# First loads on three queues, later mixing weights behind the token transposes, and engine orders from a priority table

## Chip, cores, metric

The kernel runs on one core of a Trainium2 chip. The metric is device time in microseconds (us) of one execution, as the median of several runs. A profiled execution gives, besides its own time, a span from its first to its last instruction and a record of every instruction.

## What is computed

A transformer block of two parts on 2048 tokens of width 512: linear attention with 32 heads of 16, then a gated MLP that mixes over tokens. Cut to what matters:

```python
phi = lambda t: jnp.where(t > 0, t + 1, jnp.exp(t)) + 1e-06
def _A_ref(x, wqkv, wo):
    q, k, v = ...                                  # x @ wqkv, split into heads
    pq, pk = (phi(q), phi(k))
    kv = jnp.einsum('bhsd,bhse->bhde', pk, v)
    z = jnp.einsum('bhsd->bhd', pk)
    num = jnp.einsum('bhqd,bhde->bhqe', pq, kv)
    den = jnp.einsum('bhqd,bhd->bhq', pq, z)[..., None] + 1e-06
    return (num / den) ... @ wo
def _B_ref(x, w_in, w_sp, b_sp, w_out):
    z = _gelu(jnp.einsum('bsd,df->bsf', x, w_in))
    z1 = z[..., :Fh]                               # Fh = 896
    z2 = _layernorm(z[..., Fh:], axis=-1)
    g = jnp.einsum('ts,bsf->btf', w_sp, z2) + b_sp[None, :, None]
    return jnp.einsum('bsf,fd->bsd', z1 * g, w_out)
h = x + _A_ref(_layernorm(x, axis=-1), A_wqkv, A_wo)
h2 = h + _B_ref(_layernorm(h, axis=-1), B_w_in, B_w_sp, B_b_sp, B_w_out)
```

All inputs and the output are bfloat16. The mixing weights `w_sp` are 2048 by 2048.

## The kernel before

Five engines run at once: TensorE (PE) for matmuls and transposes into PSUM, VectorE (DVE), ScalarE (ACT), GpSimd (POOL), and SyncE (SP), which here only issues transfers. Each engine takes its instructions strictly in order; an instruction whose input is not there holds up all behind it.

**Tiles and stages.** The 2048 tokens are 16 tiles of 128; two tiles are a pair, four a group. The stages are:

1. *First half.* x and the three weights wq, wk, wv (512 by 512 each) are loaded. Every tile gets its layer norm: statistics (L557) and an aggregate (L561) on DVE, Ln and Exp on ACT (L571, L573) for the inverse deviation, and the normalisation on DVE (L585) into one of four `xn` buffers. The normalised tile is transposed into `xT`: by PE, with a copy out of PSUM on ACT (L622, L627), or by a transposing transfer that SP issues (L611). `XDMA` says from which pair on it is SP. Then PE computes K and V of a pair (L654), eight matmuls of 512 columns each, and Q of a group, two feature blocks at a time (L680), eight matmuls. `phi` of K and Q is an Exp on ACT (L633) and two DVE operations (L634, L641); V is copied by ACT (L668).
2. *Sums over tokens.* 64 short matmuls (L703) give K times V and the sums of K; DVE masks and transposes them (L715 to L723), and four matmuls with wo give a combined matrix `mw` (L733).
3. *Denominators and out-projection.* The denominators of each group (L753) go through Ln and Exp on ACT, which is a reciprocal (L757, L760). They are spread over the features: by matmuls for the first group (L792), by matmuls and ACT copies into the store of the attention weights for the others (L770, L776). DVE multiplies (L796), PE multiplies with `mw` (L825), DVE adds to x (L830), which is then h.
4. *Second layer norm and z.* Statistics as above; the inverse deviation is a power on POOL (L578, L580). The first pair's tiles are transposed by PE, the other 14 by SP, into `hT`. PE computes the second half of z for each tile (L853: four matmuls of 512 and four of 384 columns), ACT applies Gelu (L862). The statistics of z are made on DVE (L877) for the tiles with `n % 4 < ZD`, and otherwise by ACT with a Square (L869) and small POOL operations. DVE normalises. The first half of z, `z1`, is computed transposed (L898), with a Gelu on ACT (L903).
5. *Mix and output.* For each of four groups of output tokens and seven feature blocks, 16 matmuls with the mixing weights (L926), then bias and gate on DVE (L932, L935); seven matmuls per tile for the output (L944), the sum with h (L950) and the store (L952).

The mixing weights come transposed from memory, by 16 transposing transfers on SP for each group (`wsp0` to `wsp3`, L504). `wsp3` uses the store of the attention weights, so it can be loaded only late. A transfer that SP issues for a token tile stands in the same queue.

**What sets the order.** Nothing is ordered by hand. Each operation is recorded with an engine, an estimated cost and a priority. `schedule` then goes through the work like a list scheduler: for each engine it computes when each ready operation could start and takes the one with the best priority among those that start at once. The order, the PSUM banks and the buffers of the pools come out of that, and waits are made for what the order needs. A constant of 0.1 us says how much later a better operation may start; every transfer is costed on its issuing engine's own queue. The scheduler's times are estimates made while building; on the chip only the order is left of them.

The loads stand in SP's queue in this order: x0, x1, wk, the pair x2 and x3, wv, and six more pairs of x; then transposes of `wsp0`. POOL loads wq after its constants, then wo, win and wout, each after the one before has landed, since POOL's transfers are chained.

Of the kernel before, what the change touches and what calls it, by code (L numbers as in the profile page):

```python
# [10 lines left out]
P = 128  # L11
# [98 lines left out]
class Program:  # L110
# [3 lines left out]
    ENGINES = ("pe", "act", "dve", "pool", "sp")  # L114

    def __init__(self, nc):
        self.nc = nc
        self.ops, self.writer, self.readers = [], {}, {}
        self.pools = {}
        self.groups = {}  # L120

    def op(self, eng, cost, fn, r=(), w=(), prio=None, after=(), dma=None, nbytes=0, lag=0.0):
# [32 lines left out]
        return o  # L155


    def _slot(self, tile):
# [14 lines left out]

    def schedule(self):
        for o in self.ops:
# [15 lines left out]
        while left:  # L191
            pick = None
            for e in self.ENGINES:
                best = None
                for o in cand[e]:
                    t = free[e]
                    for p in o.deps:
                        same = p.eng == e and p.grp is None
                        t = max(t, p.end + (0.0 if same and (e == "pe" or p not in o.raw) else 0.08))
                    self.now = t  # L200
                    ok = True
                    for tl in o.tiles:
                        if tl.slot is None:
                            s = self._slot(tl)
                            if s is None:
                                ok = False
                                break
                            t = max(t, s[2] + 0.08)
                    if not ok:
                        continue  # L210
                    key = (t if t > free[e] + 0.1 else free[e], o.prio, o.seq)
                    if best is None or key < best[0]:
                        best = (key, o, t)
                if best is not None and (pick is None or best[2] < pick[2]):
                    pick = best
# [17 lines left out]
            if o.grp is not None:  # L233
                dma_free[o.eng] = max(dma_free.get(o.eng, 0.0), t + 0.3) + o.bytes / 300e3
                o.end = max(dma_free[o.eng] + 1.2, t + 2.0)
            for tl in o.tiles:
# [119 lines left out]


def bass_sequential_preLN__linear_attn_block__mixer_gmlp__prompt_kernel(
    nc: bass.Bass,
# [19 lines left out]
    assert D == 512 and KD == 4 and NG == 4 and FH == KF * P and 512 < FH <= 1024  # L379
    WARM, XDMA, HDMA, LNACT = 10, 5, 1, 2  # L380
    DB, DC, SPP, PK, ZD = 6, 7, 14, 0.3, 1
    ONES, SCP, Q3P, NQ1 = 1, 7, 8, 4
# [104 lines left out]
    def load(eng, name, dst, src, nbytes, prio=None, whole=False, after=()):  # L487
        return op(eng, max(0.5, nbytes / 300e3) if eng == 'sp' else 0.8, lambda e: e.dma_start(dst.ap(), src), w=[dst], dma=(name, whole), nbytes=nbytes,
                  prio=prio, after=after)

    w3 = A_wqkv.rearrange("(c p) f -> p c f", p=P)
    load("sp", "x0", x[0, :], x_dram[0:P, :], P * D * 2)
    load("sp", "x1", x[1, :], x_dram[P:2 * P, :], P * D * 2)
    load("sp", "wk", wk.all(), w3[:, :, D:2 * D], D * D * 2)
    for p in range(1, NP):
        load("sp", f"x{p + 1}", x[2 * p:2 * p + 2, :],
             x_dram[2 * p * P:(2 * p + 2) * P, :].rearrange("(n p) d -> p n d", p=P), 2 * P * D * 2)
        if p == 1:
            load("sp", "wv", wv.all(), w3[:, :, 2 * D:3 * D], D * D * 2)

    def load_wsp(tg):
        for st in range(NT):
            dst = wsp[tg][st, :]
            op("sp", 1.3, lambda e, dst=dst, st=st: e.dma_start_transpose(  # L504
                dst.ap(), B_w_sp[tg * GW:(tg + 1) * GW, st * P:(st + 1) * P]),
               w=[dst], dma=(f"wsp{tg}", True), nbytes=3 * P * GW * 2, prio=5000)

    for tg in range(3):
        load_wsp(tg)

# [19 lines left out]
       r=[bmask.all()], w=[bmask.all()])  # L530


    op("pool", 0.1, lambda e: e.memset(zc.all().ap(), 0.0), w=[zc.all()])
    op("pool", 0.5, lambda e: e.memset(sel.all().ap(), 0.0), w=[sel.all()])
# [58 lines left out]
    for grp in LN1:  # L593
# [6 lines left out]
        for i, n in enumerate(grp):  # L600
            t = xn_t[n] = Tile(XN)
            o = normalise(t(), x[n, :], Row(st_x, n), 6, rs[i:i + 1], 10 * (n // 2) - 18)
            if n == 5:
                load("pool", "wq", wq.all(), w3[:, :, 0:D], D * D * 2, after=[o])
                load("pool", "wo", wo.all(), A_wo.rearrange("(c p) f -> p c f", p=P), D * D * 2, after=[o])

    def transpose_pair(p, src, dstT, prio, by_dma, single=1):
        if by_dma:
            for n in (2 * p, 2 * p + 1):
                a, d = src[n], dstT[:, n * P:(n + 1) * P]  # L610
                op("sp", 1.3, lambda e, a=a, d=d: e.dma_start_transpose(d.ap(), a().ap()), r=[a()], w=[d],  # L611
                   dma=(f"t{dstT.store.name}{n}", False), nbytes=3 * P * D * 2, prio=prio)
            return
# [300 lines left out]
    load("sp", "bsp", bsp(), B_b_sp.partition_broadcast(P), P * S * 2)  # L914
    load_wsp(3)
    G0 = Z0 + 100
# [46 lines left out]

    g.schedule()

# [53 lines left out]
```

## Time and profile before

| what | us |
|---|---|
| three runs | 253.45, 254.6, 259.03 (median 254.6) |
| the profiled execution's own time | 256.33 |
| its span, first to last instruction | 254.6 |
| first K matmul (L654) | 6.77 |
| wq lands, first Q matmul (L680) | 16.84, 16.89 |
| 64 short matmuls (L703) | 54.53 to 58.32 |
| first denominator matmul (L753) | 58.60 |
| first z matmul (L853) | 68.33 |
| last wait of PE ends; 88 z1 matmuls follow | 111.63 |
| mix begins | 130.62 |
| last output projections (L944) | 239.40 to 251.65 |

PE's clock was granted in full (1.00) throughout. The page's costliest group is the mix; its rows look like this:

```profile
L926 PE MATMUL ps<-wsp,pk_v_z 128*128 128x512 bf16 x336 | 73.0, 379 | 0.0
L633 ACT ACTIVATE e<-ps 128x1024 bf16<-128x1024 f32 x16 | 16.3, 1020 | 7.7 <-PE ps L680 4.3
```

A row has the line, the engine and operation, output and input with their shapes, the count; then busy us and the mean ns of one; then the idle time ahead of these instructions and what ended most of it. A matmul's 379 ns is its time in the pipeline; 336 of them take 73.0 us, because they overlap. The chain of waits goes back from the last instruction to whatever released it, step by step; here it is read in order of time. In the windows, each row is a stretch of time with the busy time of PE, PE's weight loads, DVE, ACT and POOL, then PE's granted clock, the share of the transfer engines in use and GB/s.

### The profile page before, as it was taken

What the parts mean: (1) busy time and instruction counts of PE and PEld (TensorE: products, weight loads), DVE (VectorE), ACT (ScalarE), POOL (GpSimd) and SP (SyncE); (2) the same over time, 40 slices, a digit from 0 to 9 for tenths busy, and PEclk for the clock granted to TensorE, in tenths of its full rate; (3) what the DMA queues carried; (4) which work ended last, traced back from release to release, by engine and by line L of the source; (5) the groups of instructions that cost most, each with busy time, mean ns of one, the idle gap of its engine ahead of it and who ended that gap; (6) DMA issues with size and microseconds to landing.
All of it is one profiled execution on the core that took longest, in us unless ns stands there. A gap on an engine that the chain in (4) does not pass through costs nothing.

```text
span 254.6 us, 3142 instructions
## 1 busy us (share of the span) xinstructions
PE 243.0 (95%) x1222; PEld 111.6 (44%) x1222; DVE 133.1 (52%) x253; ACT 89.3 (35%) x129; POOL 28.2 (11%) x74
## 2 busy tenths in 40 slices
PE   7879899999889999999999999999999999999995
PEld 3334344464334444444444444444444444444442
DVE  3797894698999799232003332243333433223443
ACT  3648655646876668897540000000000000000000
POOL 7311000001024536322000000000000000000000
PEclk9999999999999999999999999999999999999999
DMA  6979973548944454444410000002000010000022
GB/s 188 334 173 174 304 149 88 83 101 198 207 105 97 96 89 101 104 101 92 104 37 3 0 0 0 0 3 82 0 0 3 23 59 0 3 0 0 0 82 82
DMA packets 52206, 20.78 MB, mean 82 GB/s; under 512 B 46208, under 2 KB 51328, under 8 KB 52192
## 3 DMA queue, kind: packets, MB, share of 16 engines
q1 hardware_dynamic: 51392, 16.79, 31.2%
q0 software_dynamic: 800, 3.80, 5.5%
q8 instruction: 9, 0.15, 0.3%
q14 instruction: 5, 0.04, 0.1%
HBM read 7.47 MB, written 2.10 MB: 38 GB/s over the span
## 4 chain that ended last, share of the span: by engine, by line
PE 75%; DVE 11%; DMA 6%; ACT 4%; POOL 2%; issue 2%; POOLq 0%; ACTq 0%
PE ps L926 38%; PE ps L944 10%; PE ps L898 8%; PE ps L654 7%; PE ps L680 5%; PE ps L853 5%; DMA wqkv_wsp<-in_A_wqkv_dram 4%; DVE xh L830 3%; DVE small L557 3%; DMA hT<-xn 2%; DVE xT_pq_z L796 1%; ACT e L633 1%; ACT wqkv_wsp L776 1%; PE ps L622 1%; PE ps L825 1%
## 5 line engine op out<-in xcount | busy, mean ns | idle before, releaser
L926 PE MATMUL ps<-wsp,pk_v_z 128*128 128x512 bf16 x336 | 73.0, 379 | 0.0
L932 DVE TENSOR_TENSOR r<-ps,e 128x512 bf16<-128x512 f32 x28 | 19.4, 691 | 78.8 <-PE ps L926 78.8
L926 PEld LDWEIGHTS ps<-wsp,pk_v_z 128*128 128x128 bf16 x336 | 32.9, 98 | 39.6
L654 PE MATMUL ps<-wqkv_wsp,xT_pq_z 128*128 128x512 bf16 x128 | 29.2, 379 | 2.1 <-ACT xT_pq_z L627 1.0
L853 PE MATMUL ps<-win,hT 128*128 128x512 bf16 (+1 forms) x128 | 25.9, 352 | 1.5 <-DMA hT<-xn 1.1
L898 PE MATMUL ps<-hT,win 128*128 128x512 bf16 x112 | 25.0, 379 | 0.0
L944 PE MATMUL ps<-wout,xT_pq_z 128*128 128x512 bf16 x112 | 24.7, 379 | 0.0
L926 PE MATMUL ps<-wqkv_wsp,pk_v_z 128*128 128x512 bf16 x112 | 24.3, 379 | 0.0
L557 DVE BATCH_NORM_STATS2 small<-xh 128x6 f32<-128x512 bf16 x32 | 21.4, 678 | 4.7 <-DMA xh<-in_A_x_dram 4.5
L654 PEld LDWEIGHTS ps<-wqkv_wsp,xT_pq_z 128*128 128x128 bf16 x128 | 11.9, 98 | 17.7 <-ACT xT_pq_z L627 2.1
L633 ACT ACTIVATE e<-ps 128x1024 bf16<-128x1024 f32 x16 | 16.3, 1020 | 7.7 <-PE ps L680 4.3
L853 PEld LDWEIGHTS ps<-win,hT 128*128 128x128 bf16 x128 | 12.0, 97 | 15.2 <-ACT r L869 1.3
L862 ACT ACTIVATE pk_v_z<-ps 128x896 bf16<-128x896 f32 x16 | 14.6, 914 | 8.5 <-PE ps L853 6.8
L950 DVE TENSOR_TENSOR r<-ps,xh 128x512 bf16<-128x512 f32 x16 | 11.1, 691 | 11.7 <-PE ps L944 11.7
L926 PEld LDWEIGHTS ps<-wqkv_wsp,pk_v_z 128*128 128x128 bf16 x112 | 11.0, 98 | 13.2
L944 PEld LDWEIGHTS ps<-wout,xT_pq_z 128*128 128x128 bf16 x112 | 10.9, 98 | 13.2
L898 PEld LDWEIGHTS ps<-hT,win 128*128 128x128 bf16 x112 | 11.0, 98 | 12.7
L903 ACT ACTIVATE xT_pq_z<-ps 128x1024 bf16<-128x1024 f32 x14 | 14.2, 1021 | 6.5 <-PE ps L898 6.5
L680 PE MATMUL ps<-xT_pq_z,wqkv_wsp 128*128 128x512 bf16 x64 | 14.5, 379 | 1.4 <-DMA wqkv_wsp<-in_A_wqkv_dram 1.4
L825 PE MATMUL ps<-pk_v_z,xT_pq_z 128*128 128x512 bf16 x64 | 15.1, 379 | 0.6 <-ACT pk_v_z L862 0.3
L869 ACT ACTIVATE r<-pk_v_z,small 128x896 bf16<-128x896 bf16 x12 | 12.4, 1034 | 0.9 <-POOL small L867 0.9
L585 DVE TENSOR_SCALAR xn<-xh,small 128x512 bf16<-128x512 bf16 x32 | 11.7, 406 | 1.6 <-ACT small L573 0.9
(69 smaller groups left out, 180.5 us busy)
## 6 DMA issues: line engine op xcount, KB each, us to landing
out_dram<-r SPq DMA_DIRECT2D x16, 128.0 KB, 1.7
xh<-in_A_x_dram SPq DMA_DIRECT2D x7, 256.0 KB, 6.3
win<-in_B_w_in_dram POOLq DMA_DIRECT2D x1, 1792.0 KB, 8.1
wqkv_wsp<-in_A_wqkv_dram SPq DMA_DIRECT2D x2, 512.0 KB, 5.4
wout<-in_B_w_out_dram POOLq DMA_DIRECT2D x1, 896.0 KB, 6.9
wsp<-in_B_w_sp_dram SPq DMA_TRANSPOSE x48, 3.1
wqkv_wsp<-in_A_wqkv_dram POOLq DMA_DIRECT2D x1, 512.0 KB, 9.3
wqkv_wsp<-in_A_wo_dram POOLq DMA_DIRECT2D x1, 512.0 KB, 6.8
```

What stands on the lines that cost most here:

```text
L557: op("dve", dve_c(512), lambda e: e.bn_stats(s6.ap(), src.ap()), r=[src], w=[s6], prio=prio)
L633: op("act", act_c(1024), lambda e: e.activation(e_().ap(), t(flat).ap(), ACT.Exp), r=[t()], w=[e_()], prio=prio)
L654: i = e.matmul(t(bank(ti)).ap(), lhsT=lhs.ap()[:, c, :], rhs=rhs.ap()[:, c, :], start=(c == 0), stop=(c == KD - 1))
L680: r_ = e.matmul(t(bank(i)).ap(), lhsT=lhs.ap()[:, c, :], rhs=rhs.ap()[:, c, :], start=(c == 0), stop=(c == KD - 1))
L825: i = e.matmul(t(bank(ti)).ap(), lhsT=l.ap()[:, c, :], rhs=mw[c, :].ap(), start=(c == 0), stop=(c == KD - 1))
L853: k = e.matmul(t(bank(i)).ap()[:, 0:b - a], lhsT=l.ap()[:, c, :], rhs=win[c, a:b].ap(), start=(c == 0), stop=(c == KD - 1))
L862: op("act", act_c(FH, ptr=by_act), lambda e, t=t, d=d, acc={"accum_out": m.ap()} if by_act else {}: e.activation(d.ap(), t(flat).ap()[:, 0 ...
L898: k = e.matmul(t(bank(i)).ap(), lhsT=l.ap()[:, c, :], rhs=r_.ap()[:, c, :], start=(c == 0), stop=(c == KD - 1))
L903: op("act", act_c(1024), lambda e: e.activation(d.ap(), t(None if same else flat).ap(), ACT.Gelu_apprx_tanh), r=[t()], w=[d], prio=prio, a ...
L926: k = e.matmul(t(bank(0)).ap(), lhsT=l.ap()[:, s - a, :], rhs=r_.ap()[:, s - a, :], start=(s == 0), stop=(s == NT - 1))
L932: op("dve", dve_c(512), lambda e: e.tensor_tensor(gb().ap(), t(bank(0)).ap(), bsp().ap()[:, tg * GW:(tg + 1) * GW], ALU.add), r=[t(), bsp( ...
L944: k = e.matmul(t(bank(0)).ap(), lhsT=l.ap()[:, fc, :], rhs=wout[fc, :].ap(), start=(fc == 0), stop=(fc == KF - 1))
```

## The change

Four things change together.

*Loads.* x1 and wv are issued by ACT, wk by SP in two halves, wq by POOL before most of its constants. wo stays behind tile 5's normalisation.

*Mixing weights.* SP's transposes of `wsp0` and the first ten of `wsp1` may go at once; the other six and all of `wsp2` and `wsp3` come after every token transpose that SP issues.

*Constants.* Eight warm-up matmuls instead of ten; token pairs from the fifth on instead of the sixth go through SP's transposes (`XDMA` 4); z statistics of two tiles in four instead of one are made on DVE (`ZD` 2); the spread of the denominators has another priority (`SPP` 8).

*The scheduler.* Its estimates of latencies and transfers change, each engine has its own patience, and a table of 551 numbers is added to the priorities of the operations in the order in which they were recorded. The mix and the outputs lie beyond the table.

```diff
+    PATIENCE = {"pe": 0.1, "act": 0.2, "dve": 0.2, "pool": 0.1, "sp": 0.1}
...
+    @staticmethod
+    def _lag(p, o):
+
+        if p.grp is not None:
+            return 0.04
+        if p.eng == o.eng and o.grp is None:
+            return 0.0 if p.eng == "pe" or p not in o.raw else 0.11
+        return (0.2 if p.eng == "pe" else 0.11) + (0.04 if o.eng in ("pe", "pool") else 0.0)
...
-    def schedule(self):
+    def schedule(self, nudge=()):
+        for o, d in zip(self.ops, nudge):
+            o.prio += d
...
-                        same = p.eng == e and p.grp is None
-                        t = max(t, p.end + (0.0 if same and (e == "pe" or p not in o.raw) else 0.08))
+                        t = max(t, p.end + self._lag(p, o))
...
-                    key = (t if t > free[e] + 0.1 else free[e], o.prio, o.seq)
+                    key = (t if t > free[e] + self.PATIENCE[e] else free[e], o.prio, o.seq)
...
-                dma_free[o.eng] = max(dma_free.get(o.eng, 0.0), t + 0.3) + o.bytes / 300e3
-                o.end = max(dma_free[o.eng] + 1.2, t + 2.0)
+                q, b = ("all", o.bytes) if o.bytes > 0 else (o.eng, -o.bytes)
+                dma_free[q] = max(dma_free.get(q, 0.0), t + 1.0) + b / 340e3
+                o.end = dma_free[q] + 0.8
...
+NUDGE = [
...
+    0, 0, 0, 0, 0, 0, 0, 0, 0, 0, 0, 0, 0, 0, 0, 0, 0, 0, 0, 0, 0, 0, 0, 0, 0, -24.5, 27.5, -1.5, 28, -65,
+    396.5, 122.5, 93.5, 46, -45.5, -424.5, -26.5, -342, 3.5, 6.5, 17, -91, -52, -53.5, 190, -89, -15, 63.5,
...
+]
...
-    WARM, XDMA, HDMA, LNACT = 10, 5, 1, 2
-    DB, DC, SPP, PK, ZD = 6, 7, 14, 0.3, 1
+    WARM, XDMA, HDMA, LNACT = 8, 4, 1, 2
+    WSP1 = 10
+    DB, DC, SPP, PK, ZD = 6, 7, 8, 0.3, 2
...
-    load("sp", "x1", x[1, :], x_dram[P:2 * P, :], P * D * 2)
-    load("sp", "wk", wk.all(), w3[:, :, D:2 * D], D * D * 2)
+    load("act", "x1", x[1, :], x_dram[P:2 * P, :], P * D * 2, prio=-20)
+    for c in (0, 2):
+        load("sp", "wk", wk[c:c + 2, :], w3[:, c:c + 2, D:2 * D], D * D, whole=True)
...
-            load("sp", "wv", wv.all(), w3[:, :, 2 * D:3 * D], D * D * 2)
+            load("act", "wv", wv.all(), w3[:, :, 2 * D:3 * D], D * D * 2, prio=-19)
...
-    def load_wsp(tg):
-        for st in range(NT):
+    def load_wsp(tg, sts, after=()):
+        for st in sts:
...
-    for tg in range(3):
-        load_wsp(tg)
+    load_wsp(0, range(NT))
+    load_wsp(1, range(WSP1))
...
+    load_wq = load("pool", "wq", wq.all(), w3[:, :, 0:D], D * D * 2)
...
-                load("pool", "wq", wq.all(), w3[:, :, 0:D], D * D * 2, after=[o])
...
-    load_wsp(3)
+    load_wsp(1, range(WSP1, NT), by_dma_ops)
+    load_wsp(2, range(NT), by_dma_ops)
+    load_wsp(3, range(NT), by_dma_ops)
...
-    g.schedule()
+    g.schedule(NUDGE)
```

What comes out on the engines, as the built program has it. SP: x0, the halves of wk, seven pairs of x, 16 transposes of `wsp0`, tokens 8, 9, 11, 10, one transpose of `wsp1`, tokens 15, 14, 13, 12, nine of `wsp1`, the bias, the 14 transposes into `hT`, and then the remaining 38 of `wsp`. ACT: x1, wv, the table load, then Ln and Exp of tiles 0 to 3, the first Exp of phi, a copy of V, the transposes' copy of the second pair. PE: K and V of the first pair in one go, then the second pair's transposes; the first Q matmuls after four tiles of K and V as before; the K and V of tiles 8 and 9 follow K of tiles 6 and 7; eight z1 matmuls stand in the mix. DVE: both statistics of the first pair ahead of both aggregates; the normalisations of tiles 12 to 15 between the phi of tiles 4, 5 and that of tiles 6, 7, each behind the transfer of one of tiles 8 to 11, whose buffer it takes.

## The prediction

> **What bounds the kernel now.** I read the page's busy times and slices first, then the chain that ended last in order of time, then busy time by stretches, then the queue of SP.
>
> ```profile
> PE 243.0 (95%) x1222; PEld 111.6 (44%) x1222; DVE 133.1 (52%) x253; ACT 89.3 (35%) x129; POOL 28.2 (11%) x74
> PE   7879899999889999999999999999999999999995
> DVE  3797894698999799232003332243333433223443
> ```
>
> TensorE is busy 95% of 254.6 us. From slice 20 on nothing but PE counts, so all that an order can win lies before the mix. The chain dates the stages:
>
> ```profile
> 7.50 9.34 DMA wqkv_wsp<-in_A_wqkv_dram
> 16.84 0.05 issue
> 16.89 1.04 PE ps L680 x4
> ...
> 30.35 13.99 PE ps L654 x64
> 44.34 10.37 PE ps L680 x48
> ...
> 97.84 2.53 DMA hT<-xn
> 100.37 0.14 issue
> 100.51 3.19 PE ps L853 x16
> ...
> 130.79 37.99 PE ps L926 x176
> ```
>
> The last line gives 37.99/176 = 0.216 us for a 512-column matmul; 384 columns take 0.162 in proportion, and eight transposes 0.45 (L622 in the same chain). Counting the matmuls of each stage against its length gives PE's waits: 6.77 to 16.89 holds 32 matmuls and 8 transposes (7.36 us), so 2.8 are waits; 16.89 to 30.35 holds 48 and 24 (11.7), 1.7; 30.35 to 58.60 holds 112 and the 3.79 us of L703, 0.3; 58.60 to 75.12 has 4.1 and 75.12 to 111.63 1.7. Sum 10.6 us. After 111.63 PE runs on without a gap. So 10.6 us, and 0.45 for the eight transposes that leave PE, are the most the change can win. The profiled execution took 256.33, its span is 254.6 and 1.73 lie around it; the median of the three runs is 254.6. I add differences to the profiled execution and subtract the same 1.73 for the median.
>
> The new costs, patience and the table add no instruction; they set orders only.
>
> **Part 1, the three queues.** x1 and wv go to ACT's queue, wk is halved, wq goes to POOL's queue at about 3.2 us instead of 7.50. Bytes per us:
>
> ```profile
> 6.00:7.00 1.00, 0.53 (x8) 0.24 (x6) 0.00 (x0) 0.89 (x2) 0.81 (x4) 1.00 1.02 364
> 7.00:8.00 1.00, 1.00 (x6) 0.48 (x5) 0.74 (x2) 0.20 (x1) 0.93 (x3) 1.00 1.11 370
> ```
>
> With one queue in use the transfers already run at 350 to 370 GB/s (last column). Added up from the start, 1.05 MB have moved at 6.0 us; that is x0, x1, wk and the pair x2, x3, and the pair's statistics start at 7.22: 1.2 us after its last byte. If ACT's queue shares the engines, 0.52 MB of wv go in front of the pair: 1.57 MB at 7.4, landed at 8.6. If it does not share, 7.2 stays; if wq's 0.52 MB come in too, 10.0. I take 8.6, because the rate is already near its highest. (wk lands at 7.9 by the same count, 1.31 MB at 6.6 plus 1.2; the first sixteen matmuls then end at 11.4 and stay hidden below.) In the new order ACT does Ln and Exp of tiles 2, 3 (0.3 + 0.2), then the first Exp of 1.02, then the copy of V (1.02), then the copy of the transposes (1.02). Statistics and aggregates of two tiles take 1.6, so 8.6 + 1.6 + 0.55 + 3.1 = 13.8 for the second pair's matmuls, which start at 11.84 now. Sixteen of them end at 17.3, and the first Q matmul (16.89 now) no longer waits for wq: its 1.43 us of wait are gone, and 0.4 us are lost on balance (from -1.0 to +1.8). What else moves is covered: two issues of 0.43 on ACT push the 1.28 us table load to about 3, Ln is due at 4.6; wq's issue (0.98) pushes POOL's sel by a us, used at 60; wo and win behind wq on POOL's queue come sooner, used at 59 and 68.
>
> The Trainium skill, "DMA: Bandwidth & Descriptors", section "Issuing engines are not separate DMA queues", says that transfers from several engines run on the same 16 DMA engines and interleave, so that only issue time is saved. The 364 and 370 GB/s agree; by it the gain of three queues is at most the order in which things land, which is how they are priced above.
>
> Two warm-up matmuls fewer (L550, 4.45 us for ten) cost nothing by themselves: the first transposes start at about 5.7 in either case. They could cost if the clock is not up yet. The ten are 0.427 us apart, the transposes behind them run at full pace. Bounds: nothing, or 16 matmuls at 0.427 instead of 0.216, 3.4 us, of which 2.0 reach the second pair's start. I take nothing: 3.4 us of work still stand ahead.
>
> The Trainium skill, "TensorE: Matmul & The Clock Gate", Part 1, puts the warm-up at about 3.4 us of sustained work in a free-running window. By it eight matmuls just fill the window, and the gap after them is a risk.
>
> **Part 2, SP's order.** Token tiles 8 to 15 now go through SP's transposes (10 to 15 before), and all 16 transposes of wsp0 stand ahead of tile 8; before, ten stood ahead of tile 10. SP's issues now:
>
> ```profile
> 7.13 1.88 SPq L504 DMA_TRANSPOSE wsp<-in_B_w_sp_dram  x1
> 14.54 2.05 SPq L504 DMA_TRANSPOSE wsp<-in_B_w_sp_dram  x1
> 26.04 1.31 SPq L611 DMA_TRANSPOSE xT_pq_z<-xn  x1
> ```
>
> The fifth wsp transpose is issued at 14.54, and undisturbed ones follow every 1.31. So the 17th, tile 8, comes at 14.54 + 12 x 1.31 = 30.3, plus what wo and win add as they move beside it (single steps of 2.28 and 1.7 stand in the trace). Bounds: 28.9, if the fourth, at 11.87, is no longer held up by wq; 34, if all twelve take 1.62. I take 30.9, near the undisturbed row. Tiles 8, 9, 11, 10 follow every 1.31 and land 2.5 later: tile 10 at 30.9 + 3.9 + 2.5 = 37.3. The xn pool has four buffers, so DVE's normalisation of tile 12 waits for that landing, and behind it in DVE's queue stands the phi of tiles 6, 7 (0.43 + 1.23), for which PE's next Q bank waits. That is 0.37 + 1.7 + 0.1 = 2.2 us: PE goes on at 39.5 with 72 matmuls of K, V and Q left, 15.55 us, and ends them at 55.05. Now it ends them at 54.71. The whole part is worth +0.3, wherever the start stood: PE without this wait would come to the same point at 37.9: from 17.3 there are 64 matmuls and 16 transposes (14.7) and 0.7 of waits for phis to V of tile 8, then 24 matmuls (5.2). So the start is hidden behind it. The pair of transposes taken off PE (0.45) is hidden too.
>
> **Part 3, the stage from the denominators on.** I count from the first denominator matmul, 58.60 now. Its start after L703 stays (0.28 us behind). Ln, Exp, copies and phi keep their durations; walking the new order of ACT and DVE, the first z matmul comes 9.75 us in, now 9.73. Then the second Gelu table load, three spread copies and the release of one PSUM pair by the first Gelu fall a little worse: 40 out-projection and 32 z matmuls are done 23.5 us in, 22.8 now. From there on 49.2 us pass now to the mix (130.62), for 96 z (18.1), 24 out-projection (5.2) and 112 z1 matmuls (24.2): 47.5, hence 1.7 of waits. Two of these waits, 1.1 us, are for hT. Each pair of hT transposes stood behind a wsp transpose: the pair normalised by 98.8 was issued at 101.76, straight after one. With those moved behind, a tile lands 2.5 us after its normalisation, and I find every tile landed before its matmul. Eight z1 matmuls go into the mix, which costs nothing since the sum of PE's work is the same. So 23.5 + 47.5 = 71.0 against 72.0: -1.0. Against it stands ZD 2: four more tiles' Gelu statistics on DVE, 4 x 1.4 = 5.6 us, while ACT loses four squares; z1 matmuls cover it, with 0.2 us to spare at the tightest place (the bank of tiles 14, 15). Bounds: +1.0, if DVE slips by 2, and -2.5, if the early part loses nothing and more.
>
> **Part 4, the weights moved back.** 38 wsp transposes come after the last hT, at about 107. At 1.31 each wsp1 is whole at 116, wsp2 at 137, wsp3 at 158. They are needed at about 154, 184 and 205. Free, with 38 us of cover.
>
> **Sum.** +0.3 - 1.0 = -0.7 against 256.33: 255.6, and by the same 1.73, 253.9 for the median.
>
> **The rivals.** *The waits go as the table means them to.* The x pair lands at 7.2, and wsp transposes run at 1.31 from the fourth on (tile 8 issued at 28.9) or all along (6.6 + 16 x 1.31 = 27.6). Then the first half ends at 53.05 (28.9 + 24.15; -1.7) or, bound by PE's own 36.5 + 15.55, at 52.05 (-2.7). The second wins 2.5, or 4 if half of the waits from 58.60 to 75.12 go too. Together -4.2 to -6.7, near 249.2. For it: SP's plain spacing and the length of that stage's waits. Against: the trace shows the slow steps whenever loads run beside transposes, and ACT's order puts two other operations ahead of the second transposes' copy.
>
> *Tile 8 comes late* (the slower side). Place: PE at V of tile 8, DVE at the normalisation of tile 12. The first half takes 3.9 + 2.5 + 2.2 + 15.55 = 24.15 us from the issue of tile 8 on, so it loses from 30.6 on, us for us, and the whole change from 31.6. At 34 it is +3.4 - 1.0 = +2.4, 257.0. For it: five transposes took 9.5 us beside the x loads, and win now falls among them.
>
> *The clock comes up late*: +2.0 at the start, partly hidden, and DVE behind by as much: 256.
>
> *The change does little*, since PE does the same work: my forecast is nearly this.
>
> **How the numbers follow.** Forecast 0.40, waits go 0.38, tile 8 late 0.14, clock 0.08. Two per cent is 5.1 us, about what a measurement of this kernel can tell from no change. Below 249.5 lies some 0.6 of the second case: 0.23. Above 259.7 lie the tails of the last two: 0.08. Within: 0.69. The range goes from 248.6, a little below the second case's middle, to 257.4, past the late tile and the clock; the forecast's own is 252 to 255.5.
>
> **What would show it.** Right: no wait of PE for wq; PE waiting at L705 for the DMA of tile 8, between 30 and 37 us; DVE's idle time before L635 put down to an xT transpose; first denominator matmul near 59; mix (L979) near 128 with eight L949 inside it. Wrong: tile 8's transpose issued before 29 or after 33; matmuls at 0.427 after 6.8 us; waits for hT still there; gaps in the mix waiting for wsp.

## The result and the profile after

The changed kernel took 256.24 us in the median of 20 runs (255.81 to 257.76); the kernel before, run beside it, 255.81 (253.45 to 261.89, 20 runs). The kernel before has executions in a slower state as well (those from 258.86 up), so the ratio is taken over the fast runs alone and is not that of the medians: 1.006, with a 95% interval of 1.0038 to 1.0082. The change makes the kernel a little slower, by about 1.5 us, and not 0.7 us faster as forecast. The profiled execution took 256.96 us of its own time, 0.63 more than the one before, with a span of 255.2.

The changed kernel's line numbers: K and V L705 (L654 before), Q L731 (L680), the short matmuls L754 (L703), denominators L804 (L753), z L904 (L853), z1 L949 (L898), mix L979 (L926), last outputs L997 (L944), the transposes into `xT` and `hT` L662 (L611), normalisation L635 (L585), phi L684, L685 and L692. In kernels of the experiments that add lines to the scheduler, all of these are higher: by 3 with win later, by 13 and 15 where the loads are moved, by 13 where hT is moved in the new order, and by 6 in all others, hT first in the kernel before among them.

The page's busy times and the slices of PE and DVE:

```profile
PE 242.6 (95%) x1190; PEld 112.1 (44%) x1212; DVE 139.0 (54%) x265; ACT 83.1 (33%) x116; POOL 26.0 (10%) x66
PE   5879989999889999999999999999999999999995
DVE  3498968957979998875212333333323333223443
```

PE does the same work in a span 0.6 longer. A slice is 6.4 us: the first has lost two tenths against the kernel before (5 instead of 7); the others differ by a tenth here and there, too coarse to place the rest. DVE has 6 us more (the z statistics of four more tiles), and it does not matter.

The start, PE's instructions in order of time (start, length, line, shapes, count, idle time ahead and who ended it), and the window over the first sixteen K and V matmuls (the number behind POOL's is PE's granted clock):

```profile
7.89 6.38 PE L705 MATMUL ps<-wqkv_wsp,xT_pq_z 128*128 128x512 bf16 x16 [0.69 <-ACT xT_pq_z L678]
14.10 0.61 PE L673 MATMUL ps<-small,xn 128*128 128x128 bf16 x8
16.30 3.63 PE L705 MATMUL ps<-wqkv_wsp,xT_pq_z 128*128 128x512 bf16 x15 [1.58 <-ACT xT_pq_z L678]
```

```profile
8.00:14.00 6.00, 6.00 (x16) 2.16 (x15) 4.16 (x11) 1.52 (x3) 1.20 (x2) 1.00 1.44 286
```

Sixteen matmuls take 6.38 us here; the fifteen of the second pair, with one missing in the record, take 3.63. So most of the first sixteen ran at half pace, though the granted clock reads 1.00. The second pair starts at 16.30, 4.5 us later than before. The chain of waits shows what holds it up: the slow matmuls themselves, and then two copies on ACT.

```profile
7.90 6.38 PE ps L705 x16
...
14.30 1.02 ACT pk_v_z L719
15.33 0.92 ACT xT_pq_z L678
```

SP's issues, in order of time (start, length of all together, count):

```profile
7.75 25.09 SPq L553 DMA_TRANSPOSE wsp<-in_B_w_sp_dram  x16
32.88 5.19 SPq L662 DMA_TRANSPOSE xT_pq_z<-xn  x4
```

The middle of the first half, from the chain of waits in order of time:

```profile
32.96 1.74 PE ps L705 x8
...
34.78 0.72 ACT e L684
35.50 3.46 DMA xT_pq_z<-xn
...
38.98 0.41 DVE xn L635
...
39.41 0.41 DVE xn L635
39.82 0.35 DVE e L685
...
40.19 1.24 DVE pk_v_z L692
...
41.47 1.90 PE ps L731 x8
43.37 5.18 PE ps L705 x24
...
55.46 1.73 PE ps L731 x8
57.18 3.64 PE ps L754 x64
```

This is the chain that the forecast named: a token transpose, the normalisation whose buffer it frees, phi behind that, PE's next Q. Tile 8's transpose was issued at 32.88 and, by the chain, PE goes on at 41.47. PE's own idle times in this stretch are short, 0.87 and 0.16 us ahead of V and about 0.3 among the Q matmuls, since the late start had it arrive late as well. The first half ends 2.5 us later than before (first denominators at 61.08 instead of 58.60). From there to the start of the last output matmul it takes 190.8 instead of 192.7 us.

### The profile page after: what moved, and what is told of

Same layout as the page of the kernel before. It is cut to its first block, busy times and chain, and to the rows that moved or that the text cites. A ratio compares the mean times of both kernels' runs of the same rounds, so it can differ in the third digit from the quotient of the medians.

```text
span 255.2 us, 3084 instructions
## 1 busy us (share of the span) xinstructions
PE 242.6 (95%) x1190; PEld 112.1 (44%) x1212; DVE 139.0 (54%) x265; ACT 83.1 (33%) x116; POOL 26.0 (10%) x66
## 4 chain that ended last, share of the span: by engine, by line
PE 86%; DVE 5%; ACT 4%; POOL 1%; DMA 1%; issue 1%; POOLq 0%; ACTq 0%
PE ps L979 38%; PE ps L705 11%; PE ps L997 9%; PE ps L949 9%; PE ps L904 9%; PE ps L731 5%; PE ps L876 3%; PE ps L754 1%; DMA xT_pq_z<-xn 1%; DVE xT_pq_z L847 1%; DVE xn L635 1%; ACT xT_pq_z L678 1%; PE ps L673 1%; ACT wqkv_wsp L827 1%; DVE small L607 1%
## 5 line engine op out<-in xcount | busy, mean ns | idle before, releaser
L979 PE MATMUL ps<-wsp,pk_v_z 128*128 128x512 bf16 x328 | 72.8, 379 | 0.4
L979 PEld LDWEIGHTS ps<-wsp,pk_v_z 128*128 128x128 bf16 x336 | 32.9, 98 | 39.6
L705 PE MATMUL ps<-wqkv_wsp,xT_pq_z 128*128 128x512 bf16 x125 | 31.9, 406 | 3.5 <-ACT xT_pq_z L678 2.3
L954 ACT ACTIVATE xT_pq_z<-ps 128x1024 bf16<-128x1024 f32 x14 | 14.0, 1020 | 58.7 <-PE ps L949 58.6
L904 PE MATMUL ps<-win,hT 128*128 128x384 bf16 (+1 forms) x125 | 25.5, 352 | 0.5 <-ACT hT L678 0.3
L949 PE MATMUL ps<-hT,win 128*128 128x512 bf16 x109 | 25.3, 379 | 0.2
L997 PE MATMUL ps<-wout,xT_pq_z 128*128 128x512 bf16 x111 | 24.6, 379 | 0.1
L979 PE MATMUL ps<-wqkv_wsp,pk_v_z 128*128 128x512 bf16 x110 | 24.2, 379 | 0.1
L705 PEld LDWEIGHTS ps<-wqkv_wsp,xT_pq_z 128*128 128x128 bf16 x128 | 12.9, 103 | 21.0 <-issue 4.9
L684 ACT ACTIVATE e<-ps 128x1024 bf16<-128x1024 f32 x16 | 16.3, 1024 | 10.3 <-PE ps L731 4.8
L913 ACT ACTIVATE pk_v_z<-ps 128x896 bf16<-128x896 f32 x16 | 14.4, 915 | 13.8 <-PE ps L904 13.8
L904 PEld LDWEIGHTS ps<-win,hT 128*128 128x128 bf16 x128 | 12.4, 98 | 12.9 <-ACT hT L678 0.6
L997 PEld LDWEIGHTS ps<-wout,xT_pq_z 128*128 128x128 bf16 x112 | 10.9, 98 | 13.2
L979 PEld LDWEIGHTS ps<-wqkv_wsp,pk_v_z 128*128 128x128 bf16 x112 | 10.9, 98 | 13.2
L949 PEld LDWEIGHTS ps<-hT,win 128*128 128x128 bf16 x112 | 11.0, 98 | 12.6
L731 PE MATMUL ps<-xT_pq_z,wqkv_wsp 128*128 128x512 bf16 x63 | 15.2, 379 | 0.1
L635 DVE TENSOR_SCALAR xn<-xh,small 128x512 bf16<-128x512 bf16 x32 | 12.1, 405 | 4.6 <-DMA xT_pq_z<-xn 2.2
L988 DVE TENSOR_TENSOR xT_pq_z<-xT_pq_z,r 128x512 bf16<-128x512 bf16 x28 | 11.9, 425 | 1.0
```

Of the source, the lines that this page charges most:

```text
L635: return op("dve", 0.2 + 0.00026 * n, lambda e: e.tensor_scalar(dst.ap(), src.ap(), m.ap(), rs.ap(), op0=ALU.subtract, op1=ALU.mult), r=[s ...
L684: op("act", act_c(1024), lambda e: e.activation(e_().ap(), t(flat).ap(), ACT.Exp), r=[t()], w=[e_()], prio=prio)
L705: i = e.matmul(t(bank(ti)).ap(), lhsT=lhs.ap()[:, c, :], rhs=rhs.ap()[:, c, :], start=(c == 0), stop=(c == KD - 1))
L731: r_ = e.matmul(t(bank(i)).ap(), lhsT=lhs.ap()[:, c, :], rhs=rhs.ap()[:, c, :], start=(c == 0), stop=(c == KD - 1))
L904: k = e.matmul(t(bank(i)).ap()[:, 0:b - a], lhsT=l.ap()[:, c, :], rhs=win[c, a:b].ap(), start=(c == 0), stop=(c == KD - 1))
L913: op("act", act_c(FH, ptr=by_act), lambda e, t=t, d=d, acc={"accum_out": m.ap()} if by_act else {}: e.activation(d.ap(), t(flat).ap()[:, 0 ...
```

## The experiments

All runs in one table. Not all were made on the same chip, so the medians of different rows don't compare; the ratios do, since the kernel before ran beside each (its medians there: 255.26 to 257.07). The columns are the median, the ratio with its 95% interval, and, from one profiled execution each, the span, the first denominator matmul (the end of the first half), and the time from there to the start of the last output matmul (the second half).

| kernel | median us | ratio | span | first half | second half |
|---|---|---|---|---|---|
| before | 255.81 | 1 | 254.6 | 58.6 | 192.7 |
| changed | 256.24 | 1.006 [1.0038, 1.0082] | 255.2 | 61.1 | 190.8 |
| changed, run again | 256.18 | 1.0066 [1.0034, 1.0098] | 254.4 | 60.2 | 190.8 |
| ten warm-ups | 258.06 | 1.0067 [1.0025, 1.011] | 255.9 | 61.8 | 190.8 |
| tokens first | 253.51 | 0.9891 [0.9821, 0.9962] | 250.1 | 55.9 | 190.8 |
| both | 252.07 | 0.9864 [0.9799, 0.993] | 251.4 | 57.2 | 190.8 |
| both, run again | 252.71 | 0.9905 [0.987, 0.994] | 250.3 | 56.1 | 190.8 |
| both, but fourteen ahead | 254.31 | 0.9975 [0.9932, 1.0017] | 251.3 | 57.2 | 190.8 |
| both, x1 and wv on SP | 253.66 | 0.997 [0.9932, 1.0008] | 251.4 | 57.2 | 190.8 |
| the same, wq late | 252.6 | 0.993 [0.9885, 0.9975] | 252.8 | 58.7 | 190.8 |
| both, hT among wsp | 260.6 | 1.0243 [1.0159, 1.0328] | 258.9 | 57.3 | 198.3 |
| both, no table | 255.04 | 1.0029 [0.9993, 1.0065] | 252.6 | 58.3 | 191.0 |
| both, no table, again | 255.99 | 1.0018 [0.9984, 1.0052] | 252.9 | 58.7 | 190.9 |
| changed, win later | 262.8 | 1.0284 [1.0243, 1.0325] | 262.5 | 68.3 | 190.8 |
| before, eight warm-ups | 255.48 | 0.9997 [0.9955, 1.0038] | 251.5 | 56.6 | 191.7 |
| before, hT first | 253.41 | 0.9942 [0.9903, 0.998] | 252.3 | 58.0 | 191.0 |

### Ten warm-ups

```diff
-        for _ in range(WARM):
+        for _ in range(10):
```

> The changed kernel with ten warm-up matmuls in place of eight; every engine's order is otherwise that of the changed kernel. Tile theory (what sets the first half is the issue of tile 8's transpose on SP, 32.88 us, behind sixteen transposes of wsp0): the first sixteen K and V matmuls go at 0.216 us again, the second pair starts near 14.3 instead of 16.30 and the first Q near 18 instead of 19.93, but PE still goes on after tile 10's landing at about 41.5, K, V and Q still end near 57, and the time stays within 0.3 us of the changed kernel's 256.2. Clock theory (the late clock alone cost the first half): everything behind the start moves 2 us forward, PE goes on near 39.5, time near 254.2. If the slow matmuls have nothing to do with the warm-up: still 0.427 us apart, and nothing changes.

The start came as expected: the sixteen matmuls took 3.61 us and the second pair started at 13.24, three us sooner. Nothing of it was left: the ratio is that of the changed kernel. Tile 8 was issued at 32.60 all the same. PE in order of time around it, then the windows:

```profile
29.74 1.89 PE L705 MATMUL ps<-wqkv_wsp,xT_pq_z 128*128 128x512 bf16 x8
35.29 5.33 PE L705 MATMUL ps<-wqkv_wsp,xT_pq_z 128*128 128x512 bf16 x15 [3.66 <-DMA xT_pq_z<-xn]
40.46 3.62 PE L731 MATMUL ps<-xT_pq_z,wqkv_wsp 128*128 128x512 bf16 x16
```

```profile
36.00:38.00 2.00, 2.00 (x6) 0.59 (x5) 0.41 (x1) 0.00 (x0) 0.00 (x0) 0.50 0.64 70
38.00:40.00 2.00, 1.95 (x6) 0.75 (x6) 1.08 (x3) 1.02 (x1) 0.00 (x0) 0.67 0.61 128
```

A PE that arrives sooner waits 3.66 us in one piece for tile 8, and behind this wait the granted clock fell to 0.50 for 3.4 us, so the next sixteen matmuls took 5.2 us. The waiting is paid twice. The expected value within 0.3 us holds by the ratio, but with a loss in it that I had not foreseen; so this run alone does not show that the late clock is not the cause of the time. The second execution of the changed kernel, below, does.

The Trainium skill, "TensorE: Matmul & The Clock Gate", Part 1, says that the clock halves after an idle window of about 3.4 us and comes back after a busy one. In these runs it was at 0.50 behind waits of 3.66 and 6.33 us (the latter with win later, below) and stayed up behind 2.1. But it fell in a wait of 3.13 us as well (hT among the wsp transposes, below), 1.5 us after it had begun, and in that of 6.33 us it was down after 2.1 us. So a window that is idle from end to end was not needed here; the longest wait without a fall was 2.1 us, the shortest with one 3.13.

### Tokens first, alone and with ten warm-ups

```diff
         self.order = order
+        late = [o for o in order["sp"] if o.grp[0] == "wsp0"][11:]
+        sp = [o for o in order["sp"] if o not in late]
+        at = 1 + max(k for k, o in enumerate(sp) if o.grp[0].startswith("txT"))
+        order["sp"] = sp[:at] + late + sp[at:]
...
```

> The changed kernel with five of the sixteen wsp0 transposes moved behind the last token transpose on SP, so that tile 8's comes twelfth instead of seventeenth; all other orders as in the changed kernel, eight warm-ups. Tile theory: tile 8 is issued near 26 (or when it is normalised), PE no longer waits for its landing and goes on at its own pace with the late start, from V of tile 8 at 34.7 plus 5.2 us = 39.9 instead of 41.5: K, V and Q end 1.5 us sooner and the time is about 254.6. Clock theory: the late start decides, so the tokens' place is worth under 0.5 us, time about 256.

> Both edits together: ten warm-ups, and tile 8's transpose twelfth on SP. If the two hide each other (tile theory with the late clock behind it): more than the two gains added, start 2 us sooner and no wait for tile 8, PE goes on near 37.9, time about 252.7. If only the clock counts: as with ten warm-ups alone. If only the tile counts: as with the tokens moved alone, about 254.6.

Alone, with eight warm-ups, the ratio fell from 1.006 to 0.9891, about 4.3 us, more than the 1.5 expected. Part of this is that the clock came up in time here (second pair at 12.93). The chain of waits of that kernel (K and V L711, Q L737, short matmuls L760, denominators L810):

```profile
29.60 4.53 PE ps L711 x21
34.13 0.05 issue
34.18 0.59 PE ps L711 x2
34.78 3.45 PE ps L737 x16
38.23 5.18 PE ps L711 x24
...
50.32 1.73 PE ps L737 x8
52.04 3.64 PE ps L760 x64
...
55.94 0.83 PE ps L810 x12
```

Nothing but PE is left between 29.60 and the short matmuls: no transfer, no normalisation. Q ends at 52.04. With ten warm-ups it ends at 52.22 in the second execution and at 53.31 in the first, where PE waited 1.27 us for wk. The 52.04 is the 52.05 which the forecast gave as PE's own bound under "the waits go", so near by some luck: the second pair started 0.5 us later than it had there, and the 0.7 us of waits for phi that it allowed for did not come. Both edits together are not better than this one by more than the intervals (0.9864 and 0.9905 against 0.9891): with the tokens in time, two warm-ups more or fewer can't be told from nothing.

### Eight warm-ups in the kernel before

```diff
-        for _ in range(WARM):
+        for _ in range(8):
```

> The kernel before with eight warm-up matmuls in place of ten and nothing else. Clock theory: its first K matmuls go at 0.427 us as in the changed kernel; its wait for wq (1.43 us before 16.89) takes up a part of the 2 to 3 us, so the time rises by 0.5 to 1.5 us. If it is the gap behind the warm-ups of the changed kernel (1.19 us with PE idle, made by x0 and x1 landing later) and not their number: the matmuls stay at 0.216 and the time is the same within 0.3 us.

A ratio of 0.9997. In its profile there was no gap behind the warm-ups, the first twelve matmuls took 2.79 us, which is full pace, and wq landed at 14.80, so the first Q came at 14.85 instead of 16.89. The first half ended 2.0 us sooner than in the profile before, and PE's waits for hT were 0.3 instead of 1.1. Since the ratio is 1, these are differences between single executions: the profile that the forecast started from was one of this kernel's longer ones, in both halves.

### The changed kernel once more

> The changed kernel unchanged, for another profiled execution. If whether the clock is up after eight warm-ups differs from one execution to the next: the sixteen K and V matmuls may go at 0.216 here, with the second pair near 13; tile 8's transpose still sets PE at its V, near 35.5, so the time stays at 256 to 257 either way. If the late clock set the time of the first profile: a start at 0.216 comes with a time near 254.

PE's instructions in order of time:

```profile
7.56 4.82 PE L705 MATMUL ps<-wqkv_wsp,xT_pq_z 128*128 128x512 bf16 x16 [0.26 <-ACT xT_pq_z L678]
14.41 3.63 PE L705 MATMUL ps<-wqkv_wsp,xT_pq_z 128*128 128x512 bf16 x15 [1.58 <-ACT xT_pq_z L678]
```

The same program, and this time the clock came up in the middle of the sixteen (4.82 us instead of 6.38). The second pair started 1.9 us sooner, tile 8 was issued at 32.10, 0.8 sooner, and Q ended at 56.33, 0.85 sooner. So this execution gained what tile 8's issue gained and no more (256.1 us in all instead of 256.96), and the ratio over all runs is the same. The late clock is a matter of the execution, and it is hidden behind tile 8.

### Fourteen ahead of tile 8

```diff
-        late = [o for o in order["sp"] if o.grp[0] == "wsp0"][11:]
+        late = [o for o in order["sp"] if o.grp[0] == "wsp0"][14:]
```

(Ten warm-ups as well; the edit is shown against the kernel with both.)

> Ten warm-ups and fourteen of the sixteen transposes of wsp0 ahead of tile 8's, between eleven (252.1) and sixteen (258.1). Tile theory, with the price that the runs give: tile 8 is issued near 30, lands near 32.5, and PE, there at 31.6, waits for about 1 us, too short to lose the clock: time near 253 to 253.5. If the cost of the place is in proportion, 1.2 us for each transpose ahead: 255.7. If the place is not what counts: 252.1 or 258.1.

0.9975, between eleven (0.9864 and 0.9905) and sixteen (1.0067). Tile 8 was issued at 29.00. The chain of waits (line numbers as with the tokens first; SPq is SP's issuing):

```profile
31.20 1.24 DVE pk_v_z L698
32.44 0.45 SPq L668
...
32.93 2.56 DMA xT_pq_z<-xn
...
35.51 0.41 DVE xn L641
35.92 0.35 DVE e L691
...
36.29 1.24 DVE pk_v_z L698
...
37.57 1.90 PE ps L737 x8
```

The same chain as in the changed kernel, 3.9 us earlier, and with no wait long enough to lose the clock. Q ended at 53.28.

### The loads back on SP's queue

Against the kernel with both:

```diff
...
+        for n, o in (("x1", name["x1"]), ("wv", name["wv"])):
+            order["act"].remove(o)
+            o.eng = "sp"
+            at = 1 + max(k for k, q in enumerate(order["sp"]) if q.grp[0] == {"x1": "x0", "wv": "x2"}[n])
+            order["sp"].insert(at, o)
...
```

and in the second kernel also

```diff
+        order["pool"].remove(name["wq"])
+        order["pool"].insert(order["pool"].index(name["wo"]), name["wq"])
...
```

> The run with ten warm-ups and the tokens first, with x1 and wv put back on SP's queue (x1 behind x0, wv behind the pair of tiles 2 and 3); wk stays halved and wq stays early on POOL's queue. In the run without this edit PE has no wait left from the second pair's matmuls (14.20 us) to the end of Q, so the start is what sets the time there. Queue theory (ACT's queue makes x0, x1 and the pair land later): the pair's statistics come near 7.3 to 7.9 instead of 9.1, the second pair's matmuls start near 12.3, no wait for wq, and the time is 1.5 to 2 us below that run's 252.1, about 250.3. Rival (the 16 DMA engines move the same bytes in the same time, so the queue doesn't matter): time within 0.4 us of 252.1.

> As the run before it, with wq moved behind POOL's other work as well, directly ahead of wo, where it stood before the change. If wq's early issue is what part 1 of the change is worth: the pair lands at 7.2, but the first Q waits for wq to about 16.9, 1 to 1.5 us behind the run with wq early, time about 251.5. If the late wq costs nothing: same time as with wq early, within 0.4 us.

The queue theory is not borne out. With x1 and wv on SP the pair's statistics started at 6.94 in the profiled execution and, with wq late, at 8.19; with these loads on ACT's queue they started anywhere from 7.29 to 9.11 over eleven executions. So the 9.10 that the theory started from was that execution's, and no price of the queue. In the first of the two the V matmuls of the first pair waited 1.2 us for wv, and the second pair started at 14.24, against 14.20 and 13.11 with both. With wq late the pair started at 13.61 and no wait for wq shows; a wait of 1.9 us for a token transpose does, in that one execution.

By the ratios the loads on SP's queue bring no gain. With wq late the ratio (0.9885 to 0.9975) can't be told from those of both. With x1 and wv alone on SP (0.9932 to 1.0008) it lies above the first of them (up to 0.993) and barely meets the second (up to 0.994): moving these two loads to ACT may be worth 0.6 to 1%. The wait for wv would be a place for it, but the first execution with both began its second pair as late (14.20); and the runs were made on different chips. So that stays open.

### hT among the wsp transposes again, and hT first in the kernel before

```diff
+        at = [k for k, o in enumerate(order["sp"]) if o.grp[0].startswith("thT")]
+        head, ht, tail = order["sp"][:at[0]], order["sp"][at[0]:at[-1] + 1], order["sp"][at[-1] + 1:]
+        for n, k in enumerate((12, 3, 1, 1, 4, 1, 1)):
+            head += tail[:k] + ht[2 * n:2 * n + 2]
+            tail = tail[k:]
+        order["sp"] = head + tail
...
```

```diff
+        at = min(k for k, o in enumerate(order["sp"]) if o.grp[0].startswith("thT"))
+        head, tail = order["sp"][:at], order["sp"][at:]
+        ht = [o for o in tail if o.grp[0].startswith("thT")]
+        order["sp"] = head + ht + [o for o in tail if o not in ht]
...
```

> Ten warm-ups and the tokens first, and the transposes of hT put back among those of wsp on SP in the pattern of the kernel before (12 wsp behind the bias, then pairs of hT with 3, 1, 1, 4, 1 and 1 between them). If the second half gained because hT no longer stands behind wsp: waits of PE for hT of 1 to 2.5 us come back, the stretch from the first denominator to the end grows by as much, time about 253.5. If the table's order and the doubled z buffer brought it: no wait for hT, time within 0.4 us of 252.1.

> The kernel before, with the transposes of wsp that stand among those of hT moved behind the last hT on SP, and nothing else. If their order is what the second half gained by: PE's waits for hT (1.1 us in the profiled execution) go and the time falls by about 1 us (ratio 0.996). If the gain needs the table: ratio 1.000 within 0.002.

In the kernel before, this one move on SP gives a ratio of 0.9942. Its second half takes 191.0 us, that of the changed kernel 190.8, and no wait of PE for an hT transpose is left in it. Put back into the new order (the first edit, with ten warm-ups and the tokens first), the old place costs 7.5 us in the second half, three times the most expected. PE's longest waits there, and two windows:

```profile
PE ps L917 <- DMA hT<-xn: 4.4, 3, 3.1
```

```profile
106.00:110.00 4.00, 2.22 (x6) 0.87 (x7) 0.51 (x1) 0.00 (x0) 2.27 (x3) 0.52 0.53 99
110.00:114.00 4.00, 4.00 (x15) 1.76 (x14) 0.00 (x0) 0.44 (x1) 0.00 (x0) 0.62 0.45 98
```

A wait of 3.1 us for hT, and again the clock at half, from the middle of the wait to 113. The pattern is the one of the kernel before, but the new order normalises the tiles at other times, so the 7.5 us belong to this mixture and are no price of the old kernel.

### Without the table

```diff
-    g.schedule(NUDGE)
+    g.schedule()
```

> Ten warm-ups and the tokens first, with the priority table left out: the same costs, patience and parameters, hT ahead of the other wsp, and the orders that the scheduler finds without the table. If the table matters little (the hT order brought the second half, the tokens the first): time within 1 us of the run with the table, 252.1 to 253. If the table is what brings the orders up to the mix: waits of PE come back in the first half and behind the denominators, 2 to 5 us, 254 to 257.

> Ten warm-ups and the tokens first without the table once more, beside the same kernel with it. If the table counts: PE again waits some 2 us for tile 8's landing at its V, because the orders found without the table reach it earlier and put fewer Q matmuls ahead of it, and the time is 2 to 3 us above the kernel with the table, near that before. If the chips made the difference: within 1 us of the kernel with the table.

> Ten warm-ups and the tokens first once more, beside the kernel without the table on one chip. If the table brings the orders that count: 2 to 3 us below the kernel without it. If that difference lay in the chips: within 1 us of it. Against the kernel before, by the first run and by where its chain ends, a ratio of 0.986 to 0.993.

The first comparison was across chips, so both kernels were run again on one: 0.9905 with the table, 1.0018 without, 252.71 against 255.99 us. The intervals don't meet. The second halves are the same (190.8 and 190.9), so what the table gives, 3 us by the medians and 2.5 in these two executions, lies in the first. PE in order of time without the table:

```profile
17.80 7.07 PE L711 MATMUL ps<-wqkv_wsp,xT_pq_z 128*128 128x512 bf16 x31
24.71 2.75 PE L737 MATMUL ps<-xT_pq_z,wqkv_wsp 128*128 128x512 bf16 x12
29.56 3.61 PE L711 MATMUL ps<-wqkv_wsp,xT_pq_z 128*128 128x512 bf16 x16 [2.10 <-DMA xT_pq_z<-xn]
```

Without it PE does its K and V first, comes to tile 8 while tile 8 is not yet there, and waits 2.10 us; with it, Q matmuls stand between, and PE reaches tile 8 when it has landed. In the changed kernel as it stands tile 8 comes too late for either order, so the table's gain should be hidden there; no run shows that kernel without the table.

### win later

```diff
+        win_load = next(o for o in order["pool"] if o.grp is not None and o.grp[0] == "win")
+        tile8 = next(o for o in order["sp"] if o.grp[0].startswith("txT"))
+        win_load.deps[tile8] = True
```

> The changed kernel, eight warm-ups and all sixteen wsp0 transposes ahead of tile 8, with one more wait: the load of win (1.8 MB, issued at 17.78 and landed by 26.1 in the first profile) waits on POOL for tile 8's landing. If win's transfer is what stretched the steps of SP's transposes (2.56, 1.58, 1.49, 1.38 us between 18.9 and 28.3 instead of 1.31): they all go at 1.31 from the eighth on, tile 8 is issued near 29.4 to 30, and by 24.15 us from the issue to the end of Q the first half ends near 54, time near 253.5 (it lands well ahead of its use at 70). If the transposes slow down whatever runs beside them (or their number alone is to blame): tile 8 still near 32, time 256.

A miss, and a useful one. The steps of SP's transposes were 1.30 to 1.31 from the fourth on, but for one of 2.39, and tile 8 was issued at 31.09 instead of 32.88: so win's transfer does stretch them, by some 1.1 us in the first profile of the changed kernel and 2.1 in its second. (Another 0.7 us of the 1.8 was an earlier start; what makes the step of 2.39 stays open.) But now win's 1.8 MB move just when the token transposes do. The chain of waits (Q is L734), and the windows:

```profile
35.01 8.96 DMA xT_pq_z<-xn
43.98 0.09 issue
44.07 6.52 PE ps L734 x16
```

```profile
38.00:40.00 2.00, 0.00 (x0) 0.00 (x0) 0.00 (x0) 0.79 (x1) 0.00 (x0) 0.94 1.02 361
40.00:42.00 2.00, 0.00 (x0) 0.00 (x0) 0.41 (x1) 0.00 (x0) 0.00 (x0) 0.50 1.03 254
46.00:50.00 4.00, 4.00 (x11) 1.33 (x10) 2.74 (x5) 1.02 (x1) 0.00 (x0) 0.50 0.44 96
```

A token transpose that lands in 2.5 us alone took 8.96 beside win. PE waited 6.33 us for it and then ran at half pace until 50. I had asked only whether win would be there when it is used, and not what it passes on its way.

## Why the prediction was wrong, step by step

The forecast was 0.7 us less than the profile before; the profile shows 0.63 more. The difference of 1.3 is made of two terms, both with the right mechanism and the wrong size: the first half came out 2.2 worse than forecast (+2.5 instead of +0.3), the second 0.9 better.

**Tile 8's issue: the step that failed.** The forecast put it at 30.9, within bounds of 28.9 and 34, because it took the value near the undisturbed row. It came at 32.88: the fifth wsp transpose 0.5 us later than before (15.03), and the twelve steps behind it 2.1 us longer than at 1.31, some of it by win. The rest of part 2 held nearly to the tenth. It said: Q ends 24.15 us after the issue of tile 8. That gives 57.03, 56.25 and 53.15 for the issues at 32.88, 32.10 and 29.00; measured were 57.18, 56.33 and 53.28. (With ten warm-ups and an issue at 32.60 it ended at 57.89, 1.1 later than this sum, by the clock that the wait had lowered.) With the tokens first PE's own chain takes over and ends at 52.04. So the rival "tile 8 comes late" was the case that came true. I had its price right (2.3 us for 32.88 over 30.6) and its chance, 0.14, too low. The trace of before had shown five transposes take 9.5 us beside loads, and I named win as the load that would now fall among them; that was the reason to take a later value.

**The second half: -1.9 instead of -1.0.** The reason was right: behind 40 out-projection and 32 z matmuls the new order shows none of the 1.7 us of waits that I counted out. What failed is the loss of 0.7 that I set against them: these matmuls were done 22.7 us in, not 23.5. The move of wsp behind hT alone gives nearly all of the gain (before: 192.7, with that move 191.0). But part of the -1.9 is the profile that it is counted from: the second half of the kernel before took 191.7 in the execution with eight warm-ups, while the new order took 190.84, within 0.01 us, in ten profiles. Counted from 191.7 it is -0.8. The z statistics on DVE cost nothing that shows.

**Part 1.** The second pair started at 16.30 instead of 13.8, 2.5 us late. The pair's statistics came at 9.10 (forecast 8.6), but they were not what held it up: the chain runs through the sixteen slow matmuls, 2.75 us longer than at full pace; my bound for that, 2.0 on the pair's start, was too low. In the other executions with these loads the second pair started between 12.93 and 14.41. From there PE's own chain to the end of Q takes 39.1 us with the tokens in time (12.93 to 52.04); from 16.30 that is 55.4, so in this execution tile 8 still came 1.8 us later than the late start by itself. That the start is hidden behind tile 8 held: 1.9 us in one execution, 3.1 with ten warm-ups, gained no measurable time. The price of nothing for two warm-ups was right in time, and wrong in its reason: not that the clock was up, but that it was hidden. No gain from the early wq could be told from nothing.

**Part 4.** No wait for wsp in the mix; eight z1 matmuls stand in it. Free, as forecast.

**The offset.** I took 1.73 us off for the median, as the profile before stood above it. That belonged to that kernel's spread. The changed kernel's own profile stands 0.7 above its median. The forecast of 253.9 is off by 2.3: 1.3 from the terms above and 1.0 from this. The median lies in the range all the same.

**The rivals.** "The waits go" comes nearest to what this order can do when SP's queue lets it: 252 to 253 us, not the 249.2 at which I put it. Its condition, tile 8 issued by about 28, was what the change itself broke, with sixteen transposes of wsp ahead of it. The clock rival named 256 for a reason that another execution of the same program shows not to set the time. `XDMA` 4, which put tiles 8 and 9 on SP's queue in the first place, `ZD`, `SPP` and the scheduler's new costs had no run of their own.

A version faster than both kernels comes out of this: the changed kernel with ten warm-ups and eleven transposes of wsp0 ahead of the tokens, 252.07 and 252.71 us in two sets of runs, ratios of 0.9864 [0.9799, 0.993] and 0.9905 [0.987, 0.994].

## What to carry to other kernels

An order found by search is as good as its costs on the queue that nobody counts as an engine: here 1.31 us per transposing issue, and up to 2.8 in single steps while loads ran, decided between a gain of 1% and a loss of 0.6%. Where a chain has a clean formula and one uncertain input, the spread of that input is the forecast; take its middle from the disturbed rows if the disturbance will be there. And before a transfer is moved to a free place, look at what it passes there, not only at when it is needed.

## What was not expected of the hardware

- *A wait of PE is paid twice once it is long enough.* With idle times of 3.66, 6.33 and 3.13 us the granted clock went to 0.50: for 3.4 us in the first case, from 39.8 to 50 in the second, and from 106.2 to 113 in the third; behind 2.1 us it stayed at 1.00. It is part of why ten warm-ups gained nothing and of the 7.5 us that hT in the wrong place cost.
- *The same program starts at a different pace.* With eight warm-ups the first sixteen matmuls took 6.38, 4.82, 3.63 and 3.61 us in four profiled executions of kernels that begin alike; with ten, 3.6 us where the sixteen ran in one piece, in every profile. The granted clock reads 1.00 in all of them: at the start it has to be read off the matmuls' spacing.
- *A transposing transfer beside a plain load takes much longer.* A token transpose took 8.96 us beside a load of 1.8 MB and 2.5 without, and with that load moved away SP's issues of transposes lost 1.1 and 2.1 us of what they had taken beyond 1.30 us each.
